# Spreading GpSimd's gathers and scatters over the expert items by due dates

## The chip, the cores and the metric

The kernel runs on one core of a Trainium2 chip. The metric is the device time of one execution in microseconds (us); three executions were timed, and their median is compared. A profiled execution gives the trace: what each engine did, and when. TensorE is PE, VectorE is DVE, ScalarE is ACT, GpSimd is POOL; SP only issues DMAs here.

## The reference, cut to what matters

Attention over 4 batches, 8 heads, 768 positions and 64 elements, in which a query sees the keys of its own cluster, is followed by a mixture of eight experts with one expert for each of the 3072 tokens:

```python
expert_idx = np.argmax(logits, axis=1)
gate_w = probs[np.arange(N), expert_idx]
for e in range(E):
    mask = expert_idx == e
    h = np.maximum(x[mask] @ w1[e], 0.0)
    out[mask] = gate_w[mask, None] * (h @ w2[e])
```

x has 512 columns, w1 is 512 x 1024 and w2 1024 x 512 for each expert, all in fp32.

## The kernel before, in words

The first half (to about 360 us) is attention. It writes x to DRAM (`x_rows`) and finds each token's expert and a place for it. The change touches only what follows: the experts.

The tokens are dealt to *items*, each with one expert's weights. Four "early" items (`E0`) take tokens of the first batches, 128 rows each. The list `later` has 16 more: later[0] is a "block" (128 rows), later[1] and later[2] are "sized", then block and sized alternate (sized ones are 1, 2, 4, 6, 8, 10, 12, 14), and later[15] is a block. The eight sized items hold up to 272, 256, 240, 224, 208, 192, 176 and 160 tokens (`CAPS`), in that order. Overflow items stand behind a branch (`overflow`) that is not taken with these inputs.

One item goes through these steps:

- **Weights.** `weights1` and `weights2` (L1117 to L1131) load w1 and w2, 2 MB each, on SP's queue into one of two buffers each, two items ahead.
- **Gather** (`fetch`, L1133). POOL issues indirect DMAs from `x_rows`, each of 128 pieces of 128 elements. A sized item has WIDE[j] of them (9, 8, 8, 7, 7, 6, 6, 5) into `xs` (two buffers), a block has four into `xin` (three buffers). The instruction is at L1079 inside `gather`.
- **Turn** (`turn_x`). DVE transposes `xs` to `xTs` (L1177) or `xin` to `xTm` (L1186).
- **Hidden.** `sized_hidden` (L1207): eight groups of matmuls (L1217) into PSUM banks, three of h_ps and one of x_ps (groups 4 and 8), each group evicted by ACT with a Relu to `hTs` (L1224). For a block `hidden` does it in two halves (L1303, L1310).
- **Result.** `sized_result` (L1243): four groups of matmuls (L1254) against `w2o`, a copy of w2 in another order that DVE made before (`order_w2`, L1202). DVE transposes each group into `ys` (L1263), and then multiplies `ys` by the gates in place (L1277). A block's result (L1319) is scaled by ACT to `y` (L1330), and POOL scatters it to `out` with one DMA.
- **Send** (`send`, L1281). POOL scatters a sized item's `ys` to `out` with WIDE[j] indirect DMAs (L1090 inside `scatter`). `ys` has two buffers.

Each engine runs its instructions in the order in which the program emits them; nothing is reordered. The loop at the end of the kernel (L1600 to L1642) writes that order by hand. In iteration i it turns the activations of later[i + 1], issues all gathers of later[i + 2] if that is sized, then the scatters of later[i - 1], then emits the hidden part of later[i]. The gathers of a following block wait on POOL behind a one-element copy (`pace`, L1628) of the last hidden group. Of the scatters of a sized item before a block, the first three (`RUN`) are issued at once, the rest behind a copy of the block's last hidden element (L1598). So POOL works in rows of seven to thirteen DMAs.

Of the kernel before, what the change touches and what calls it, by code (L numbers as in the profile page):

```python
# [9 lines left out]
F32 = mybir.dt.float32  # L10
# [8 lines left out]
P = 128  # L19

SQ = 32
# [18 lines left out]
def kernel(  # L40
# [12 lines left out]
    nc = tc.nc  # L53
# [4 lines left out]
    F = moe_w1.shape[2]  # L58
    N = B * S
# [5 lines left out]
    KF = F // P  # L65
    NQ = P // SQ
# [9 lines left out]
    WIDE = [-(-c // SQ) for c in CAPS]  # L76
    FIRST = [sum(WIDE[:i]) for i in range(E)]
# [1 line left out]
    NB = NS + KX  # L79


    RUN = 3
    MORE = (2, 4, 8)
    NO = sum(MORE)
    assert -(-(N - P - min(CAPS)) // P) <= KX + NO and min(CAPS) >= P
# [8 lines left out]
    x_pieces = x_rows.rearrange("n (w x) -> (n w) x", w=NQ)  # L94
    out_pieces = out.rearrange("n (w x) -> (n w) x", w=NQ)
# [57 lines left out]
    at = ctx.enter_context(ExitStack())  # L153
# [922 lines left out]
    mo = {}  # L1076

    def gather(to, of, at, n):
        nc.gpsimd.indirect_dma_start(  # L1079
            out=to,  # L1080
            out_offset=None,
            in_=of,
            in_offset=bass.IndirectOffsetOnAxis(ap=at, axis=0),
            bounds_check=n - 1,
            oob_is_err=False,
        )

    def scatter(to, at, of, n):

        inst = nc.gpsimd.indirect_dma_start(  # L1090
            out=to,
            out_offset=bass.IndirectOffsetOnAxis(ap=at, axis=0),
            in_=of,
            in_offset=None,
            bounds_check=n - 1,
            oob_is_err=False,
        ).ins
        tc.declare_no_dep(
            inst, group="out", reason="a row of out is written by one slot of one item"
        )  # L1100
        tc.add_to_no_dep_group("out", inst)
# [16 lines left out]
    def weights1(it, parts=1):  # L1118
        it.e = expert_of(it)
        for i in range(parts):  # L1120
            load_part(w1s[it.slot], moe_w1, it.e, KD, i, parts)

    def weights2(it, parts=1):
        for i in range(parts):
            load_part(w2s[it.slot], moe_w2, it.e, KF, i, parts)
# [4 lines left out]
            out=w[:, c], in_=x[ds(e, 1)].rearrange("o (c p) f -> p (o c) f", p=P)[:, c]  # L1130
        )  # L1131

    def fetch(it, a=0, z=None):  # L1133
        if a == 0:
            mo[it] = {}
        if it.kind == "sized":
            u0, n = FIRST[it.j], WIDE[it.j]
            if a == 0:
                mo[it]["xs"] = szp.tile([P, max(WIDE), P], F32, tag="xs", name="xs")
            xs = mo[it]["xs"]  # L1140
            for u in range(n)[a:z]:
                gather(xs[:, u], x_pieces, flat(gpidx)[:, u0 + u : u0 + u + 1], NQ * N)
            return
        if it.kind == "whole":
            xin = mo[it]["xin"] = it.xin
            gather(
                xin.rearrange("p w x -> p (w x)"), x_rows, it.tables[1][:, it.col : it.col + 1], N
            )
            return
        xin = mo[it]["xin"] = xip.tile([P, NQ, P], F32, tag="xin", name="xin")  # L1150
        if it.kind == "early":
            n = SA * P
            gather(
                xin.rearrange("p w x -> p (w x)"), x_rows[0:n], gidxs[0][:, it.j : it.j + 1], n
            )
            return
        for w in range(NQ):
            gather(xin[:, w], x_pieces, it.tables[0][:, it.col, w : w + 1], NQ * N)

    def fetch_gate(it):  # L1160
        gate = mo[it]["gate"] = xip.tile([P, 1], F32, tag="gatein", name="gatein", bufs=4)
# [42 lines left out]
                w2s[it.slot][:, f].rearrange("p (w g i) -> p g w i", w=NQ, i=SQ),  # L1204
            )

    def sized_hidden(it):  # L1207

        d, C = mo[it], CAPS[it.j]
        d["hT"] = szp.tile([P, KF, max(CAPS)], F32, tag="hTs", name="hTs", bufs=1)  # L1210
        for f in range(KF):
            if f % 4 == 3:
                bk = psX.tile([P, DM], F32, tag="x_ps", name="x_ps")[:, 0:C]
            else:
                bk = psH.tile([P, 512], F32, tag="h_ps", name="h_ps")[:, 0:C]
            for c in range(KD):
                nc.tensor.matmul(  # L1217
                    bk,
                    lhsT=w1s[it.slot][:, c, P * f : P * f + P],
                    rhs=d["xT"][:, c, 0:C],  # L1220
                    start=(c == 0),
                    stop=(c == KD - 1),
                )
            nc.scalar.activation(d["hT"][:, f, 0:C], bk, ACTF.Relu)  # L1224

    def spread_gates():

# [15 lines left out]
    def sized_result(it):  # L1243

        d, C, n = mo[it], CAPS[it.j], WIDE[it.j]
        ys = d["ys"] = szp.tile([P, max(WIDE), P], F32, tag="ys", name="ys")
        cut = KF - 2
        bks = {}

        def products(g, fs):  # L1250
            if g not in bks:
                bks[g] = misc() if g >= 2 else bank("y_ps", psY)
            for f in fs:
                nc.tensor.matmul(  # L1254
                    bks[g][:, 0:C],
                    lhsT=d["w2"][:, f, P * g : P * g + P],
                    rhs=d["hT"][:, f, 0:C],
                    start=(f == 0),
                    stop=(f == KF - 1),
                )  # L1260
# [12 lines left out]
        for g in range(2, KD):  # L1273
            products(g, range(KF))
            turn_back(g)
        u0 = FIRST[it.j]
        nc.vector.tensor_tensor(  # L1277
            ys[:, 0:n], ys[:, 0:n], bc(flat(gates4)[:, u0 : u0 + n], [P, n, P], 2), ALU.mult
        )

    def send(it, a=0, z=None):  # L1281

        u0, n = FIRST[it.j], WIDE[it.j]
        for u in range(n)[a:z]:
            at = flat(spidx)[:, u0 + u : u0 + u + 1]
            scatter(out_pieces, at, mo[it]["ys"][:, u], NQ * N)
        if z is None:
            del mo[it]

    def flat(t):  # L1290
        return t.rearrange("p k w -> p (k w)")
# [141 lines left out]
    with tc.manual_schedule(engines=by_hand):  # L1433
# [104 lines left out]
        gates = gate_pieces(B - 1, B)  # L1538
        gates[0]()
        result(E0[1], (1,))  # L1540
        pb.pieces(gpidx, spidx)
        fetch(later[0])
        pb.token_rows(None, sidxs[1])
# [50 lines left out]

        LAST = len(later) - 1

        def wait_hidden(it, f):
            nc.gpsimd.tensor_copy(pace, mo[it]["hT"][0:1, f : f + 1])  # L1598

        for i, it in enumerate(later):  # L1600
            if i == LAST - 1:
                overflow()
                weights1(later[LAST])
                weights2(later[LAST])
            if it.kind == "sized":
                order_w2(it)
            if i + 1 < len(later):
                turn_x(later[i + 1])
            if i > 0 and i + 2 < len(later) and later[i + 2].kind == "sized":
                fetch(later[i + 2])  # L1610
            late = i > 0 and later[i - 1].kind == "sized" and it.kind == "block" and i < LAST
# [4 lines left out]
            if it.kind == "sized":  # L1616
# [6 lines left out]
            if i == 0:  # L1623
                pb.gates(slot_gates)
            for j in range(i + 2, min(i + 4, len(later))):
                if later[j].kind == "block" and later[j] not in mo:
                    if it.kind == "sized":
                        nc.gpsimd.tensor_copy(pace, mo[it]["hT"][0:1, KF - 1, 0:1])  # L1628
                        fetch(later[j])
            if i + 2 < LAST:  # L1630
                weights1(later[i + 2])
                if it.kind == "sized":
                    weights2(later[i + 2])
            if it.kind == "sized":
                sized_result(it)
            else:
                result(it)
            if i == 0:
                fetch(later[2])
                spread_gates()  # L1640
            if i + 2 < LAST and it.kind != "sized":
                weights2(later[i + 2])  # L1642
        if later[-1].kind == "sized":
            send(later[-1])


# [41 lines left out]
```

## Time and profile before

| what | us |
|---|---|
| three executions | 699.18, 702.19, 703.92; median 702.19 |
| the profiled execution, its own time | 699.54 |
| its span in the trace | 697.7 |
| PE busy | 684.7 |
| POOL busy | 252.7 |
| POOL: 56 gathers to xs, 32 gathers to xin | 56.6 and 32.6 |
| POOL: 56 scatters of ys, 12 of y | 56.3 and 12.0 |
| POOL: copies to pace, 6 at L1598 and 7 at L1628 | 1.3 and 1.2 |

In the page's rows, "out<-in xcount | busy, mean ns | idle before, releaser" tells what a group of instructions writes and reads, how often, how long in all and on average, and how long its engine had been idle ahead of it, with what ended that. POOL's bar for an indirect DMA ends when the engine is done with issuing; the data lands later. In the table by stage each row gives a stage's limits and length, the busy time of PE, PE's weight loads, DVE, ACT and POOL (instructions in brackets), the granted PE clock, the share of time in which DMA engines were busy, and GB/s.

### The profile page before, as it was taken

How to read it: one execution, taken by the hardware profiler on the slowest of the kernel's cores; microseconds unless marked ns; L12 is line 12 of the kernel's file. 1: busy time of each engine (PE TensorE's matmuls, PEld its weight loads, DVE VectorE, ACT ScalarE, POOL GpSimd, SP SyncE). 2: the span in 40 equal slices, each digit the busy share in tenths (PEclk: the TensorE clock that was granted, in tenths of full speed). 3: DMA queues.
4: the chain of work that ended last, by engine and by line, in shares of the span. 5: the costliest groups of instructions: out<-in, count | busy, mean ns of one | idle time of the engine just before them, and what ended most of it. 6: DMA issues, size and time to landing. Idle time of an engine off the chain costs nothing.

```text
span 697.7 us, 16185 instructions
## 1 busy us (share of the span) xinstructions
PE 684.7 (98%) x6517; PEld 459.1 (66%) x6517; DVE 381.4 (55%) x667; ACT 261.5 (37%) x443; POOL 252.7 (36%) x439
## 2 busy tenths in 40 slices
PE   8999999999999999999999999998999999999996
PEld 4444444444444444456776678887979797979694
DVE  6788998998899999988563121240210303030310
ACT  5656655577666765576142120101010111111111
POOL 2122222321132222361216256736364554635402
PEclk9999999999999999999999999999999999999999
DMA  8755566875578587699699957457777686879450
GB/s 136 121 90 108 103 98 82 163 142 104 107 134 165 122 154 149 173 277 260 171 357 353 348 172 284 158 192 244 260 249 268 218 296 236 294 265 317 143 226 32
DMA packets 244156, 135.55 MB, mean 194 GB/s; under 512 B 207840, under 2 KB 207842, under 8 KB 244076
## 3 DMA queue, kind: packets, MB, share of 16 engines
q1 hardware_dynamic: 237116, 121.10, 63.9%
q0 software_dynamic: 6016, 13.12, 5.2%
q8 instruction: 54, 0.88, 0.6%
q10 hardware_dynamic: 944, 0.23, 0.2%
q14 instruction: 26, 0.21, 0.1%
HBM read 115.92 MB, written 13.12 MB: 185 GB/s over the span
## 4 chain that ended last, share of the span: by engine, by line
PE 89%; issue 4%; DMA 3%; POOL 1%; DVE 1%; another core or an unknown queue 1%; POOLq 0%; ACT 0%; DVEq 0%
PE s_ps L519 22%; PE o_ps L541 18%; PE h_ps L1303 10%; PE y_ps L1319 10%; PE h_ps L1217 9%; PE y_ps L1254 5%; PE misc L1254 5%; PE x_ps L1217 3%; DMA out_dram<-ys,spidx 3%; PE misc L591 2%; PE misc L412 2%; PE misc L670 1%; POOL out_dram L1090 0%; POOL xin L1079 0%
## 5 line engine op out<-in xcount | busy, mean ns | idle before, releaser
L530 ACT ACTIVATE prob<-s_ps 128x768 f32<-128x768 f32 x192 | 154.1, 814 | 100.8 <-PE s_ps L519 99.9
L519 PE MATMUL s_ps<-qT,kT 64*64 64x384 f32 x1536 | 155.6, 482 | 0.0
L541 PE MATMUL o_ps<-prob,v 64*64 64x385 f32 x1536 | 141.2, 483 | 0.0
L560 DVE TENSOR_TENSOR acc<-acc,prob 128x768 f32<-128x768 f32 x128 | 121.6, 950 | 8.5
L541 PEld LDWEIGHTS o_ps<-prob,v 64*64 64x64 f32 x1536 | 58.4, 133 | 65.0 <-issue 57.8
L1263 DVE STREAM_TRANSPOSE ys<-y_ps 128x256 f32<-128x256 f32 (+4 forms) x16 | 6.5, 414 | 156.8 <-PE y_ps L1254 141.1
L1303 PE MATMUL h_ps<-xTm,w1s 128*128 128x128 f32 x768 | 89.0, 276 | 1.2 <-issue 1.2
L1303 PEld LDWEIGHTS h_ps<-xTm,w1s 128*128 128x128 f32 x768 | 87.6, 192 | 3.0 <-issue 2.6
L1319 PE MATMUL y_ps<-w2s,hT 128*128 128x512 f32 x192 | 84.5, 593 | 0.0
L1090 POOL DMA_INDIRECT out_dram<-ys,spidx x56 | 56.3, 1005 | 74.7 <-DVE ys L1277 58.7
L519 PEld LDWEIGHTS s_ps<-qT,kT 64*64 64x64 f32 x1536 | 55.2, 133 | 36.9 <-issue 32.3
L1217 PE MATMUL h_ps<-xTs,w1s 128*128 128x272 f32 (+7 forms) x384 | 72.9, 346 | 1.1 <-ACTq L1577 1.1
L1217 PEld LDWEIGHTS h_ps<-xTs,w1s 128*128 128x128 f32 x384 | 66.6, 190 | 8.0 <-issue 2.4
L575 POOL COPY behind<-acc 1x1 f32<-1x1 f32 x30 | 6.7, 223 | 177.9 <-DVE acc L560 169.1
L1310 ACT ACTIVATE hT<-h_ps 128x512 f32<-128x512 f32 x24 | 14.3, 596 | 146.1 <-PE h_ps L1303 136.3
L519 PE MATMUL s_ps<-hot 64*64 64x384 bf16 x768 | 64.2, 325 | 1.0 <-DVE hot L478 0.7
L1079 POOL DMA_INDIRECT xs<-x_rows,gpidx x56 | 56.6, 1010 | 17.1 <-issue 16.8
L1319 PEld LDWEIGHTS y_ps<-w2s,hT 128*128 128x128 f32 x192 | 35.6, 190 | 40.2 <-issue 40.2
L519 PEld LDWEIGHTS <-hot 64*64 64x64 bf16 x768 | 23.8, 106 | 43.8 <-issue 41.8
L1254 PE MATMUL y_ps<-hTs,w2o 128*128 128x272 f32 (+7 forms) x256 | 48.2, 346 | 0.2 <-issue 0.2
L1254 PE MATMUL misc<-hTs,w2o 128*128 128x272 f32 (+7 forms) x256 | 48.0, 346 | 0.0
L1254 PEld LDWEIGHTS y_ps<-hTs,w2o 128*128 128x128 f32 x256 | 44.4, 190 | 2.9 <-issue 0.4
(273 smaller groups left out, 694.9 us busy)
## 6 DMA issues: line engine op xcount, KB each, us to landing
w1s<-in_moe_w_dram SPq DMA_DIRECT2D x18, 2048.0 KB
w2s<-in_moe_w_dram SPq DMA_DIRECT2D x18, 2048.0 KB
v<-in_v_dram SPq DMA_DIRECT2D x128, 48.0 KB
k<-in_k_dram SPq DMA_DIRECT2D x62, 96.0 KB
q<-in_q_dram SPq DMA_DIRECT2D x60, 96.0 KB
x_rows<-xb SPq DMA_DIRECT2D x60, 96.0 KB
xr<-x_rows SPq DMA_DIRECT2D x9, 512.0 KB
w1s<-in_moe_w_dram SPq DMA_DIRECT2D x4, 1024.0 KB
```

Of the source, the lines that this page charges most:

```text
L412: nc.tensor.matmul(bk[2 * C * i : 2 * C * i + 2 * C, 0:HS], lhsT=cnB[:, hp], rhs=r, start=True, stop=True,)
L519: nc.tensor.matmul(s_ps[D * half : D * half + D, h, 0:HS], lhsT=l[rows, half], rhs=r[rows], start=part == (1 if len(parts) < 2 else 0), st ...
L530: nc.scalar.activation(d["prob"][:, :, 0:HS], d["s_ps"][:, :, 0:HS], ACTF.Exp, scale=scale)
L541: nc.tensor.matmul(g["o_ps"][D * h : D * h + D, half, 0:HE], lhsT=ld[n]["v"][keys, j, h], rhs=d["prob"][keys, h, 0:HE], start=(j == 0), st ...
L560: nc.vector.tensor_tensor(g["acc"], g["acc"], d["prob"][:, :, 0:HS], ALU.add)
L1079: nc.gpsimd.indirect_dma_start(out=to, out_offset=None, in_=of, in_offset=bass.IndirectOffsetOnAxis(ap=at, axis=0), bounds_check=n - 1, oo ...
L1090: inst = nc.gpsimd.indirect_dma_start(out=to, out_offset=bass.IndirectOffsetOnAxis(ap=at, axis=0), in_=of, in_offset=None, bounds_check=n - 1,
L1217: nc.tensor.matmul(bk, lhsT=w1s[it.slot][:, c, P * f : P * f + P], rhs=d["xT"][:, c, 0:C], start=(c == 0), stop=(c == KD - 1),)
L1254: nc.tensor.matmul(bks[g][:, 0:C], lhsT=d["w2"][:, f, P * g : P * g + P], rhs=d["hT"][:, f, 0:C], start=(f == 0), stop=(f == KF - 1),)
L1303: nc.tensor.matmul(bk[:, m : m + P], lhsT=w1s[it.slot][:, c, f0 + m : f0 + m + P], rhs=d["xT"][:, P * c : P * c + P], start=(c == 0), stop ...
L1310: nc.scalar.activation(d["hT"][:, f0 : f0 + 512], bk, ACTF.Relu)
L1319: nc.tensor.matmul(bk, lhsT=d["hT"][:, P * c : P * c + P], rhs=w2s[it.slot][:, c], start=(c == 0), stop=(c == KF - 1),)
```

## The change

A list `queue` takes the place of the fixed rows. `fetches(it)` and `sends(it)` return one small job for each DMA instead of issuing them, and each job goes into the queue with a due date, the number of an iteration. The gathers of later[i + 2], if sized, and of the blocks later[i + 2] and later[i + 3] are due in iteration i; the scatters of later[i - 1] are due in i + 1. `share(i, left, x)` is called seven times in a sized item (after hidden groups 2, 4, 6 and 8, and after result transposes 1, 2 and 3) and three times in a block (ahead of the hidden part and after each half). It issues the number of due jobs divided by the chances left in this item, or a smaller share of all jobs if that is more. `pump` puts one copy of an element of x (of `hTs`, `hT` or `ys`) into `pace` on POOL ahead of the lot. The last iterations send the rest. The parts of later[1] and later[2] are queued in the same way, the former among the early items.

The core of the diff:

```diff
-    RUN = 3
...
+    def fetches(it):
+
+        d = mo.setdefault(it, {})
+        if it.kind == "sized":
+            to, u0 = szp.tile([P, max(WIDE), P], F32, tag="xs", name="xs"), FIRST[it.j]
+            d["xs"], at, n = to, flat(gpidx)[:, u0:], WIDE[it.j]
+        else:
+            to = d["xin"] = xip.tile([P, NQ, P], F32, tag="xin", name="xin")
+            at, n = it.tables[0][:, it.col], NQ
+        return [
+            lambda u=u: gather(to[:, u], x_pieces, at[:, u : u + 1], NQ * N) for u in range(n)
+        ]
...
             nc.scalar.activation(d["hT"][:, f, 0:C], bk, ACTF.Relu)
+            then(f, d["hT"][0:1, f, 0:1])
...
+            then(g, ys[0:1, 0, SQ * g : SQ * g + 1])
...
+        def pump(n, behind=None):
+            if n and queue and behind is not None:
+                nc.gpsimd.tensor_copy(pace, behind)
+            queue.sort(key=lambda j: j[0])
+            for due, job in queue[0:n]:
+                job()
+            del queue[0:n]
+
+        def share(i, left, behind=None):
+
+            due = len([j for j in queue if j[0] <= i])
+            pump(max(-(-due // left), -(-len(queue) // (left + 3))), behind)
...
-        fetch(later[1], 0, NQ)
+        for job in jobs_of(later[1], 0)[0:NQ]:
+            job()
         result(E0[2])
-        fetch(later[1], NQ)
+        pump(2)
         weights2(later[0])
         turn_x(later[0])
         result(E0[3])
+        pump(1)
...
             if i > 0 and later[i - 1].kind == "sized":
-                send(later[i - 1], 0, RUN if late else None)
-                if i == LAST:
-                    nc.gpsimd.drain()
-            if it.kind == "sized":
-                sized_hidden(it)
+                made = mo[later[i - 1]]["ys"][0:1, 0, 0:1]
+                queue.extend((min(i + 1, LAST - 2), f) for f in sends(later[i - 1]))
+            if 0 < i < LAST - 1 and later[i + 2].kind == "sized":
+                jobs_of(later[i + 2], i)
+            for k in range(i + 2, i + 4):
+                if wide and block(k) and later[k] not in mo:
+                    jobs_of(later[k], i)
+            if wide:
+                sized_hidden(it, lambda f, x: share(i, 7 - f // 2, x) if f % 2 else None)
...
+                sized_result(it, lambda g, x: share(i, 3 - g, x) if g < 3 else None)
+            elif i < LAST:
+                share(i, 3, made)
+                hidden(it, (0,))
+                share(i, 2, mo[it]["hT"][0:1, 511:512])
+                hidden(it, (1,))
+                share(i, 1, mo[it]["hT"][0:1, F - 1 : F])
...
             else:
+                pump(len(queue))
+                nc.gpsimd.drain()
                 hidden(it)
-            if late:
-                wait_hidden(it, F - 1)
-                send(later[i - 1], RUN)
...
-                    if it.kind == "sized":
-                        nc.gpsimd.tensor_copy(pace, mo[it]["hT"][0:1, KF - 1, 0:1])
-                        fetch(later[j])
```

More of the change, by code (lines that the diff above doesn't have):

```diff
@@ L1131, in load_part, with fetch @@
         )
-    def fetch(it, a=0, z=None):
-        if a == 0:
-            mo[it] = {}
-        if it.kind == "sized":
[L1137 to L1143, printed above, removed]
+    def fetch(it):
+        mo[it] = {}
         if it.kind == "whole":
@@ L1205, in order_w2, with sized_hidden @@
             )
-    def sized_hidden(it):
+    def sized_hidden(it, then=lambda f, x: None):
         d, C = mo[it], CAPS[it.j]
@@ L1241, in spread_gates, with sized_result @@
         nc.vector.tensor_tensor(gates4, gates4, parts[:, 2], ALU.add)
-    def sized_result(it):
+    def sized_result(it, then=lambda g, x: None):
         d, C, n = mo[it], CAPS[it.j], WIDE[it.j]
@@ L1279, in sized_result, with sends @@
         )
[L1281 to L1288, printed above, removed]
+    def sends(it):
+        u0, ys = FIRST[it.j], mo.pop(it)["ys"]
+        return [
+            lambda u=u: scatter(
+                out_pieces, flat(spidx)[:, u0 + u : u0 + u + 1], ys[:, u], NQ * N
+            )
+            for u in range(WIDE[it.j])
+        ]
     def flat(t):
@@ L1540, with jobs_of @@
         result(E0[1], (1,))
+        queue = []
+        def jobs_of(it, due):
+            jobs = fetches(it)
+            queue.extend((due, f) for f in (jobs[NQ:] if due == 0 else jobs))
+            return jobs
+        def pump(n, behind=None):
[8 more added lines that the diff above has]
+            pump(max(-(-due // left), -(-len(queue) // (left + 3))), behind)
         pb.pieces(gpidx, spidx)
@@ L1595, with block @@
         LAST = len(later) - 1
-        def wait_hidden(it, f):
-            nc.gpsimd.tensor_copy(pace, mo[it]["hT"][0:1, f : f + 1])
+        def block(k):
+            return k <= LAST and later[k].kind == "block"
         for i, it in enumerate(later):
@@ L1604 @@
                 weights2(later[LAST])
-            if it.kind == "sized":
+            wide = it.kind == "sized"
+            if wide:
                 order_w2(it)
-            if i + 1 < len(later):
+            if i > 1 and i + 1 < len(later):
                 turn_x(later[i + 1])
-            if i > 0 and i + 2 < len(later) and later[i + 2].kind == "sized":
-                fetch(later[i + 2])
-            late = i > 0 and later[i - 1].kind == "sized" and it.kind == "block" and i < LAST
+            made = None
@@ L1612 @@
             if i > 0 and later[i - 1].kind == "sized":
-                send(later[i - 1], 0, RUN if late else None)
-                if i == LAST:
-                    nc.gpsimd.drain()
-            if it.kind == "sized":
-                sized_hidden(it)
-            else:
+                made = mo[later[i - 1]]["ys"][0:1, 0, 0:1]
+                queue.extend((min(i + 1, LAST - 2), f) for f in sends(later[i - 1]))
+            if 0 < i < LAST - 1 and later[i + 2].kind == "sized":
+                jobs_of(later[i + 2], i)
@@ new lines @@
+            for k in range(i + 2, i + 4):
+                if wide and block(k) and later[k] not in mo:
+                    jobs_of(later[k], i)
+            if wide:
+                sized_hidden(it, lambda f, x: share(i, 7 - f // 2, x) if f % 2 else None)
+                if i == 1:
+                    turn_x(later[2])
+                if i + 2 < LAST:
+                    weights1(later[i + 2])
+                    weights2(later[i + 2])
+                sized_result(it, lambda g, x: share(i, 3 - g, x) if g < 3 else None)
[5 more added lines that the diff above has]
+                share(i, 1, mo[it]["hT"][0:1, F - 1 : F])
+                if i == 0:
+                    turn_x(later[1])
+                    pb.gates(slot_gates)
+                if i + 2 < LAST:
+                    weights1(later[i + 2])
+                result(it)
+                if i == 0:
+                    jobs_of(later[2], 1)
+                    spread_gates()
+                if i + 2 < LAST:
+                    weights2(later[i + 2])
+            else:
+                pump(len(queue))
+                nc.gpsimd.drain()
@@ L1619 @@
                 hidden(it)
-            if late:
-                wait_hidden(it, F - 1)
-                send(later[i - 1], RUN)
[L1623 to L1627, printed above, removed]
-                        nc.gpsimd.tensor_copy(pace, mo[it]["hT"][0:1, KF - 1, 0:1])
-                        fetch(later[j])
[L1630 to L1633, printed above, removed]
@@ L1634 @@
-            if it.kind == "sized":
-                sized_result(it)
-            else:
-                result(it)
[L1638 to L1644, printed above, removed]
+                result(it)
 _INS = [
```

## The prediction

> **What bounds the kernel now.** I read the page first, then the busy time by stage, then what TensorE (PE) waited for stage by stage, and last the timeline of the one place where it waited. The first row of the page, and two stages of the expert part from the table by stage:
>
> ```profile
> PE 684.7 (98%) x6517; PEld 459.1 (66%) x6517; DVE 381.4 (55%) x667; ACT 261.5 (37%) x443; POOL 252.7 (36%) x439
> ```
>
> ```profile
> 440.00:473.00 33.00, 33.00 (x170) 27.12 (x170) 8.45 (x19) 2.73 (x6) 18.93 (x21) 1.00 0.58 208
> 473.00:516.00 43.00, 40.87 (x211) 34.79 (x210) 7.63 (x16) 4.53 (x11) 20.88 (x24) 1.00 0.68 236
> ```
>
> The second number after the stage is its length, the third PE's busy time. PE is idle for 13.0 us of the 697.7 us span. About 6.3 of these lie around the last matmuls (660 to 698), 1.16 at 389 to 392 (PE's own issue), 1.1 at the branch of the overflow (659.4 to 660.5). GpSimd (POOL) is about half busy in the expert part, so what the change reorders is not the bound; it matters only where something it feeds reaches PE late. The chain of waits runs through POOL from 636 us on; there I follow PE instead, which works on without a gap, because POOL waits there for DVE and ACT. All waits of PE from 402 to 660:
>
> ```profile
> PE x_ps L1217 <- ACT hTs L1224: 2.1, 1, 2.1
> PE y_ps L1254 <- issue: 0.2, 1, 0.2
> ```
>
> The 2.1 us are in later[4], a sized item. Timeline of ACT, POOL and PE there (start, duration, then idle time before it):
>
> ```profile
> 475.37 0.37 ACT L1224 ACTIVATE hTs<-h_ps 128x240 f32<-128x240 f32 x1 [0.99 <-issue]
> 478.82 0.37 ACT L1224 ACTIVATE hTs<-h_ps 128x240 f32<-128x240 f32 x1 [3.08 <-PE h_ps L1217]
> 482.42 0.37 ACT L1224 ACTIVATE hTs<-h_ps 128x240 f32<-128x240 f32 x1 [3.23 <-PE h_ps L1217]
> 486.70 0.37 ACT L1224 ACTIVATE hTs<-x_ps 128x240 f32<-128x240 f32 x1 [3.91 <-remote]
> ...
> 475.95 1.04 POOL L1079 DMA_INDIRECT xs<-x_rows,gpidx  x1 [0.30 <-issue]
> ...
> 483.83 1.00 POOL L1079 DMA_INDIRECT xs<-x_rows,gpidx  x1 [0.30 <-issue]
> ...
> 487.12 1.89 PE L1217 MATMUL x_ps<-xTs,w1s 128*128 128x240 f32 x8 [2.13 <-ACT hTs L1224]
> ```
>
> PE had finished the first four of the eight hidden groups at 475.3, 476.9, 478.5 and 480.1 (eight matmul records, 1.62 us, each). ACT evicts the first at once, the next three 1.9, 3.9 and 6.6 us late, and the eighth group, which needs x_ps back, stops PE. ACT catches up 1.9 us after the last of seven gathers in a row, issued while the w2s load of 473.68 runs. In later[6] the same happens (gathers 518.3 to 527.2, ACT up to 5.5 us late, free at 529.1), where the buffers hide nearly all of it. In later[1], with gathers but the load over by 408, ACT is on time; so it is beside the 438 to 449 scatters. What delays it I cannot see; that it goes with a long row of gathers inside a weight load I can.
>
> [...] a gather issued at 385.67 to 386.67 beside w2s loads was turned by DVE at 392.98, 6.3 us on, and one that ended at 415.12 on idle queues at 416.75, 1.6 us on. [...] so POOL's 1.0 us bars say nothing of landing. [...] Here a scatter beside w2o's copies takes 1.12 us instead of 0.97; the trace decides, so I price it at 0.15.
>
> **The change part by part.** In after's instruction order PE, DVE, ACT and SP keep every instruction in place; only POOL's order changes. Matmuls, bytes and SP's weight loads stay.
>
> *Removed:* seven waits on hTs and six on hT with their bursts behind. *Added:* 68 pace copies for 13, so 55 more: 0.18 us each, with the idle time beside it about 0.6, 33 us of POOL in 300. A DMA costs POOL 1.3 us from start to start (1.00 + 0.30). In the worst pair of items, later[4] and [5], there are 23 DMAs and 10 copies: 23 x 1.3 + 10 x 0.6 = 36 us in the pair's 42.3 (473.49 to 515.82). In the last pair, [12] and [13], 19 and 10: 31 in 34.2. POOL keeps up; cost on PE 0. Without that cover each us too much per pair would add itself.
>
> *Moved gathers.* I replayed POOL with these prices against the trace's ACT and DVE times. The ninth gather of later[1] goes from 386.98 to behind hT of later[0] (ACT ends at 392.2), so it ends about 394.4 instead of 387.98. At the 6.2 us that it took before it lands at 400.6; DVE turns it (0.31), then its four gate operations (0.9) end at 401.8. PE needs the gates' copy at 402.20 and xTs at 402.41. Cost 0 with 0.6 to 1.5 us in hand, bound 0 to +3. later[2]'s last gather ends at 421.3 instead of 415.1, beside the w1s and w2s loads of 417.4; with 3 to 6 us of landing, 425 to 428, before 431.85. For the other items the last xs gather ends 5 us or more ahead of DVE's turn.
>
> *New wait.* ys is read by the pace copies, and the gate multiply (L1277) writes ys in place, so it now also waits for POOL. In the replay the copy behind the third transpose runs at 464.5 for later[2] and 506.6 for later[4]; the multiply was here:
>
> ```profile
> 460.16 1.22 DVE L1277 TENSOR_TENSOR ys<-ys,gates 128x1024 f32<-128x1024 f32 x1
> 461.30 1.30 DVE L1177 STREAM_TRANSPOSE xTs<-xs 128x512 f32<-128x512 f32 x2
> ```
>
> So it slips 4.4 and 4.1 us, in later items 1 to 2. Queued behind it on DVE are the transpose to xTs (1.3), w2o (2.9) and xTm (0.7); later[4]'s xTs is ready at about 467.1 and PE wants it at 473.5, later[6]'s at 508.9 for 515.8. Slack 6.4 and 6.9 us, later 9 to 10. PE's banks come free by the transposes ahead of the multiply. Cost 0, hidden by the block item's 14 us; bound 0 to +7.
>
> *The lag of ACT.* In later[4]'s hidden part POOL now issues six scatters, and its seven xs gathers move to 493 and after, into the result part, where a late DVE has slack. In later[6] about three DMAs fall before the eighth group, mostly scatters. So I take the 2.1 us and the 0.2 away: -2.4 us with the 0.1 by which x_ps matmuls are stretched. Bounds: 0 (the lag moves with the traffic) to -5, if the other executions, 2.65 us above the profiled one, hold more of it. I take -2.4, the amount the trace shows.
>
> *Tail.* later[13] sends all that is left; later[14] and [15] issue as before, the drain included. Cost 0.
>
> Sum: 697.7 - 2.4 = 695.3 us of span, with the 1.84 us around it (699.54 - 697.7) 697.1 for a profiled execution. The median of the runs, 702.19, is 2.65 above the profiled 699.54; I keep that distance: **699.8 us**.
>
> **Rivals.** *No gain:* scatters and gathers still share the DMA engines with the loads, and every sized item still has POOL work in its hidden part; the lag comes up elsewhere or stays. For it: DVE was 4.9 us late in later[2]'s result part as well, beside four gathers. Against it: scatters alone left ACT on time. 702.2 us. It includes that the change spreads less than it says: POOL is so full around 460 to 510 that lots run into each other. *First gather late:* the ninth gather needs 9 us instead of 6.2; PE starts later[1] up to 3 us late, 705.2 us. *Slower, by the new wait:* POOL's copies wait for ACT and DVE and inherit their lag. The multiply of later[2] may slip 6.4 us more before PE stops; one lag of 6.6 us, ACT's worst, costs 0.2, two in one result part 13.2 - 6.4 = 6.8 us, which gives 709.0 us. Each further pair that does so adds as much. Against it: slack grows to 9 to 10 us later. *More gain:* all of the 2.65 us goes too, 697.1 us or, with the 1.16 at 389 to 392, 695.9.
>
> **How the numbers follow.** Chances: my forecast 0.52, no gain 0.27, first gather late 0.09, slower by the wait 0.07, more gain 0.05. The range is 695.5 to 706.0: the forecast with its bound of -5 at the lower end and the spread of the runs (699.18 to 703.92), no gain and the late gather inside, the slower case left out. Beyond 1% (7 us), about what a measurement of this kernel can tell from no change, on the fast side would take more than the idle time of PE that the change can reach (2.4 + 1.2 + 1.1 = 4.7) and something unseen besides: 0.04, taken out of the more-gain case. On the slow side the wait's case and a little of the late gather: 0.08. Within: 0.88. The forecast itself lies within 1%.
>
> **What would show it.** Right: in the waits of PE the line for hTs is gone or under 1 us; ACT's evictions in later[4] and [6] follow PE by 0.1 us; the multiply at L1277's place waits for a POOL copy by 2 to 5 us in later[2] and [4], and PE goes from item to item without a gap. Wrong: a wait of PE for the transposes of xs or for the gates' copy before later[1] (the first gather), one for xTs at 473 or 516 (the new wait), or ACT late by 4 us and more in other sized items (no gain). A time under 695 or over 709 would say that my reading of PE as the bound missed a stage.

## The result, and the profile after

| what | before | after |
|---|---|---|
| executions, us | 701.07 median (697.60 to 703.92, 6 runs) | 694.87 median (694.68 to 695.32, 6 runs) |
| profiled execution, its own time, us | 699.54 | 695.09 |
| its span in the trace, us | 697.7 | 693.3 |
| POOL: pace copies; busy us | 13; 252.7 | 68; 266.2 |

The changed kernel takes 0.9923 of the time before, 95% interval [0.9896, 0.9951]: 6.2 us less, 4.9 below the predicted 699.8 and a little below the range, but inside 1%. Its executions lie 0.64 us apart, those of the kernel before 6.3. The kernel before takes 694.5 us in some sessions and 696 to 702 in others (a session is a set of runs made one after the other on one chip), so each experiment below stands beside runs of the kernel before from its own session. The chip doesn't tell these sessions apart: e9 and e11, in one of each kind, both ran on the one numbered 15. One of the four runs of e12 (720.66 us), 1.6% above the fastest of its kernel, is left out of its numbers.

The first row of the page after, and the two stages shown of before:

```profile
PE 684.1 (99%) x6517; PEld 459.3 (66%) x6517; DVE 381.8 (55%) x667; ACT 262.6 (38%) x443; POOL 266.2 (38%) x494
```

```profile
440.00:473.00 33.00, 33.00 (x170) 26.97 (x169) 7.76 (x16) 3.03 (x6) 20.80 (x28) 1.00 0.61 218
473.00:516.00 43.00, 43.00 (x226) 37.64 (x226) 7.51 (x16) 5.56 (x13) 27.05 (x35) 1.00 0.73 258
```

PE's busy time is nearly the same (684.7 and 684.1); of the 4.4 us by which the span is shorter, 3.8 are idle time of PE. From 473 to 516 PE was busy 40.87 us of 43 and is now busy all 43. In that stage POOL has more to do than before (27.05 us for 20.88). All waits of PE from 360 us to the end of the span:

```profile
PE h_ps L1220 <- ACTq L1605: 1.1, 1, 1.1
```

That is the branch of the overflow, there before as well. The wait for hTs and the small one of y_ps are gone. ACT in later[4]'s hidden part, from the timeline:

```profile
475.24 0.37 ACT L1227 ACTIVATE hTs<-h_ps 128x240 f32<-128x240 f32 x1 [1.19 <-PE h_ps L1220]
476.86 0.37 ACT L1227 ACTIVATE hTs<-h_ps 128x240 f32<-128x240 f32 x1 [1.25 <-PE h_ps L1220]
478.48 0.37 ACT L1227 ACTIVATE hTs<-x_ps 128x240 f32<-128x240 f32 x1 [1.25 <-PE x_ps L1220]
...
486.46 0.37 ACT L1227 ACTIVATE hTs<-x_ps 128x240 f32<-128x240 f32 x1 [2.75 <-remote]
```

The evictions follow at PE's step of 1.62 us; only the eighth comes late, by 1.5 us. "remote" is a release that the trace has no record of. ACT is not on time everywhere: in the block later[7] the first half is evicted 2.6 us late, which lengthens that part on PE by 0.1 us:

```profile
542.30 0.60 ACT L1316 ACTIVATE hT<-h_ps 128x512 f32<-128x512 f32 x1 [17.91 <-remote]
```

The gain has a second part that I had not forecast, ahead of later[1]. PE in later[0]'s hidden part, before and then after:

```profile
385.42 4.07 PE L1303 MATMUL h_ps<-xTm,w1s 128*128 128x128 f32 x35
389.95 0.27 PE L1303 MATMUL h_ps<-xTm,w1s 128*128 128x128 f32 x1 [0.46 <-issue]
390.68 0.49 PE L1303 MATMUL h_ps<-xTm,w1s 128*128 128x128 f32 x2 [0.46 <-issue]
391.40 3.16 PE L1303 MATMUL h_ps<-xTm,w1s 128*128 128x128 f32 x26 [0.24 <-issue]
```

```profile
385.56 7.31 PE L1309 MATMUL h_ps<-xTm,w1s 128*128 128x128 f32 x64
```

The same 64 matmuls took 9.1 us (385.42 to 394.56) and take 7.3. So later[1] starts on PE at 400.7 instead of 402.4 (1.7 us), later[6] at 511.7 instead of 515.8 (2.4 more), later[14] at 656.0 instead of 660.5 (0.4 more). That is the 4.4 us of the spans.

### The profile page after: what moved, and what is told of

It is laid out like the page before. It is cut to its first block, busy times and chain, and to the rows that moved or that the text cites. A ratio compares the mean times of both kernels' runs of the same rounds, so it can differ in the third digit from the quotient of the medians.

```text
span 693.3 us, 16291 instructions
## 1 busy us (share of the span) xinstructions
PE 684.1 (99%) x6517; PEld 459.3 (66%) x6517; DVE 381.8 (55%) x667; ACT 262.6 (38%) x443; POOL 266.2 (38%) x494
## 4 chain that ended last, share of the span: by engine, by line
PE 91%; issue 3%; DMA 3%; POOL 1%; DVE 1%; POOLq 0%; ACT 0%; DVEq 0%
PE s_ps L518 22%; PE o_ps L540 18%; PE h_ps L1309 10%; PE y_ps L1325 10%; PE h_ps L1220 9%; PE y_ps L1258 6%; PE misc L1258 5%; PE x_ps L1220 3%; DMA out_dram<-ys,spidx 3%; PE misc L590 2%; PE misc L411 2%; PE misc L669 1%; PE idle_ps L232 1%; POOL xin L1078 0%; POOL out_dram L1089 0%
## 5 line engine op out<-in xcount | busy, mean ns | idle before, releaser
L1258 PEld LDWEIGHTS misc<-hTs,w2o 128*128 128x128 f32 x256 | 44.4, 190 | 2.7 <-issue 0.2
```

The costliest lines, as they stand in the source:

```text
L1258: nc.tensor.matmul(bks[g][:, 0:C], lhsT=d["w2"][:, f, P * g : P * g + P], rhs=d["hT"][:, f, 0:C], start=(f == 0), stop=(f == KF - 1),)
```

## The experiments

Lateness of ACT or DVE is worked out from the trace: start of the eviction or transpose less the end of PE's group. A "row" is a run of POOL's indirect DMAs with less than 0.6 us from the end of one to the start of the next, counted in POOL's timeline. "The lag" is the lateness of ACT, DVE and PE that the kernel before shows in some sessions.

### e1 to e4: four ways to part the change, in a session without the lag

e1 is the kernel before with the xs gathers of later[4] and each sized item after it taken out of the hidden part and put behind a copy of the last hidden group:

```diff
             if i + 1 < len(later):
                 turn_x(later[i + 1])
-            if i > 0 and i + 2 < len(later) and later[i + 2].kind == "sized":
-                fetch(later[i + 2])
...
             if i == 0:
                 pb.gates(slot_gates)
+            if i > 0 and i + 2 < len(later) and later[i + 2].kind == "sized":
+                nc.gpsimd.tensor_copy(pace, mo[it]["hT"][0:1, KF - 1, 0:1])
+                fetch(later[i + 2])
```

> The kernel before, with one edit: the gathers of the sized item two ahead are issued in one row behind the last hidden group instead of ahead of the first. Rows stay long (seven gathers, then the four of the block), nothing is spread, the row among the early items stays. Theory (place): a row of gathers inside a weight load holds up the engines beside it, and it costs only where PE depends on ACT soon, in the hidden part; moved out of it, ACT is on time (0.1 us) in later[4] and later[6], the 2.4 us of PE's idle time there go, the 1.2 to 1.8 us at later[0] stay, and DVE is late by up to 5 us in the result parts instead. Span about 695, time 0.3 to 0.7% below before. Rival (length of the row): only short lots cure it; with eleven in a row it gets worse, ACT or DVE late by 5 us or more, PE waits again for hTs or for xTs: no gain, within 0.2% of before.

e2 is the kernel before with these gathers left in the hidden part, but in lots of two behind every second hidden group:

```diff
+            then(f)
...
-            if i > 0 and i + 2 < len(later) and later[i + 2].kind == "sized":
-                fetch(later[i + 2])
...
+                def lot(f):
+                    if f % 2 and i > 0 and i + 2 < len(later) and later[i + 2].kind == "sized":
+                        nc.gpsimd.tensor_copy(pace, mo[it]["hT"][0:1, f, 0:1])
+                        fetch(later[i + 2], f - 1, f + 1)
+
+                sized_hidden(it, lot)
```

> The kernel before, with one edit: the gathers of the sized item two ahead stay in the hidden part but go out in lots of two, each behind a copy of hidden group 2, 4, 6 or 8. Theory (place): inside the w2 load of the block it is the same traffic at nearly the same time, so ACT is still late by 2 us or more in later[4] or later[6], and PE still waits for hTs: within 0.3% of before. Rival (length of the row): lots of two behind ACT cannot run ahead of it, ACT is late by under 1 us, PE's wait for hTs is gone: 0.3 to 0.7% below before.

e3 is the changed kernel with later[1]'s last five gathers in one row again (`pump(2)` becomes `pump(len(queue))`, the `pump(1)` goes):

> The changed kernel, but with the gathers of later[1] as before: four, then five in one row ahead of the scatter of the last early item. Theory: the gaps of PE in later[0]'s hidden part (1.8 us in the trace of before, none in that of the changed kernel) come from that row; they are back, span 694.5 to 695.5, time 0.2 to 0.3% above the changed kernel, and the spread of its runs grows. Rival: the gaps came by chance and not by that row: span 693.3 as in the changed kernel.

e4 is the kernel before without the loads of w2 for later[5], [7], [9], [11] and [13]; it leaves these weights out, so part of the computation works on old ones:

```diff
-            if i + 2 < LAST and it.kind != "sized":
+            if i + 2 < LAST and it.kind != "sized" and i < 3:
                 weights2(later[i + 2])
```

> The kernel before, but the w2 of the block items later[5], [7], [9], [11] and [13] is not loaded (their results are computed with the w2 that is in the buffer); these five loads ran beside the hidden part of a sized item. Rows of gathers stay. Theory (a row of gathers hurts only inside a weight load): ACT is on time, within 0.2 us, in the hidden parts of later[4] to later[12], and PE's wait for hTs is gone: span about 695, 0.3 to 0.5% below before. Rival (the row alone does it, without a load): ACT is late by 2 us or more in later[4] and later[6] as before, and the time within 0.2% of it.

Measured: before 694.50 (41 runs); e1 694.43, ratio 1.0 [0.9992, 1.0009]; e2 694.52, 0.9999 [0.999, 1.0007]; e3 694.61, 1.0 [0.9992, 1.0009]; e4 694.30, 0.9996 [0.9987, 1.0004]. Here the kernel before had no lag to lose, so none of the four tells the theories apart. They do show two things: without the lag the order of POOL's work is worth nothing either way, to 0.1%, and the changed kernel's 694.87 us has nearly reached the 694.5 of the kernel before without the lag. As e4 met no lag, the part of the weight loads stays untested by it.

### e5 and e6: the changed kernel again, and rows made longer

e5 is the changed kernel as it is. e6 is the kernel before with the first four gathers of later[4] and of each sized item after it issued twice, the second time into a spare tile; these rows grow by four, no weight load moves:

```diff
+            if it.j >= 2:
+                again = szp.tile([P, NQ, P], F32, tag="again", name="again", bufs=1)
             for u in range(n)[a:z]:
-                gather(xs[:, u], x_pieces, flat(gpidx)[:, u0 + u : u0 + u + 1], NQ * N)
+                at = flat(gpidx)[:, u0 + u : u0 + u + 1]
+                gather(xs[:, u], x_pieces, at, NQ * N)
+                if it.j >= 2 and u < NQ:
+                    gather(again[:, u], x_pieces, at, NQ * N)
```

> The changed kernel once more, unaltered, beside the kernel before. In the four runs ahead of this one the kernel before took 694.5 us instead of 701.1, with no late ACT in the traces beside it, so what held it up was not there. Theory (the change only takes away the exposure to a lag that is there at some times or on some chips): where the kernel before takes 697 us or more, this one is 0.5 to 1% below it; where it takes 694.5, the two agree within 0.1%. Rival (the change takes a constant amount): 0.4% or more below before in either case.

> The kernel before, but the first four gathers of later[4] and of each later sized item are issued twice, the second time into a spare tile: rows of nine to twelve DMAs instead of five to eight at the start of the hidden part, the result unchanged. Theory (a row only hurts where the lag is there): where the kernel before takes 694.5 us, nothing, within 0.15%, since PE waits for nothing on POOL; where it takes 697 us or more, ACT is late for longer and the time is 0.3% or more above it. Rival (the length of the row makes the lag by itself): ACT is late by 2 us or more in the hidden parts in either case, and PE waits for hTs.

Measured: before 701.71 (698.25 to 703.15, 7 runs); e5 694.92 (694.79 to 695.19), ratio 0.9909 [0.9876, 0.9942]; e6 729.13 (727.08 to 730.55), ratio 1.0386 [1.0348, 1.0424]. PE's largest waits in e6 from 360 us on, and the worst place (ACT, then PE):

```profile
PE h_ps L1222 <- issue: 10.2, 1, 10.2
PE x_ps L1222 <- issue: 5.7, 2, 3.5
PE y_ps L1259 <- issue: 3.3, 5, 0.9
PE h_ps L1222 <- ACT hTs L1229: 1.8, 1, 1.8
```

```profile
448.36 0.38 ACT L1229 ACTIVATE hTs<-h_ps 128x256 f32<-128x256 f32 x1 [30.88 <-remote]
```

```profile
436.73 1.89 PE L1222 MATMUL x_ps<-xTs,w1s 128*128 128x256 f32 x8
448.80 3.78 PE L1222 MATMUL h_ps<-xTs,w1s 128*128 128x256 f32 x8 [10.18 <-issue]
```

PE had finished this first hidden group at 433.4; ACT evicts it 14.9 us later, and the second one 18.8 us late. PE's fifth group needs a bank of h_ps back and starts at 448.80, as this eviction ends. A row of 16 gathers ran on POOL from 418 to 438.8, and nine scatters after a pause of 0.94 us. From 432 to 450 no weights were being loaded; the queue of SP (q1) beside that of POOL (q0) in the table of DMA queues for this stretch (packets, MB, share of the 16 engines' time):

```profile
q0 software_dynamic: 434, 0.87, 15.7%
q1 hardware_dynamic: 5, 0.01, 0.1%
```

So the largest lateness in all traces falls where no weight load runs, and a pause of 0.94 us does not end it once it is there. That a load has no part in it isn't shown: this row ran beside one up to 432, and so did every row longer than nine in the traces with the lag for about half of its time or more (worked out from q1's packets). The rows of nine that ran without a load, all of scatters (e6, e11 and e12), had engines at most 1.2 us late beside them in e11 and e12; in e6 the lag was there already. Two dozen more DMAs (six items of four) cost 27 us, with POOL busy for 275.3 us of a span of 728.7.

### e7, e8, e9: again without the lag

e7 is e2, e8 is e1 once more. e9 is the changed kernel without its copies to pace: queue and due dates stay, so the lots run into one another.

```diff
         def pump(n, behind=None):
-            if n and queue and behind is not None:
-                nc.gpsimd.tensor_copy(pace, behind)
             queue.sort(key=lambda j: j[0])
```

> The kernel before with the gathers of the sized item two ahead kept in the hidden part, in lots of two behind hidden groups 2, 4, 6 and 8, once more: on the chip of the first try the kernel before had no lag to cure. With doubled rows, on a chip where it has, ACT was 15 us late while SP's queue was empty, so a weight load is not needed; the length of GpSimd's rows is my theory now. Theory (row length), where the kernel before takes 697 us or more: ACT is late by under 1 us in later[4] and later[6], PE's wait for hTs is gone, time 0.4 to 0.9% below before, though the gathers stay in the hidden part. Rival (place): ACT late by 2 us or more there, within 0.3% of before. Where the kernel before takes 694.5 us neither is told apart.

> The kernel before with the same gathers in one row of up to twelve behind the last hidden group, once more. Theory (row length), where the kernel before takes 697 us or more: the lag is as large or larger than in before, now in the result part: DVE or ACT late by 3 us or more there, PE partly held up, time from 0.5% below to 1% above before. Rival (place): the lag is harmless there, 0.4 to 0.9% below before, as the changed kernel.

> The changed kernel without the copies to pace: the same lots in the same order, but GpSimd issues them as soon as it reaches them, so they run together into rows and run ahead into the hidden part. Theory (rows without a pause make the lag), where the kernel before takes 697 us or more: ACT is late by 2 us or more in some sized item, 0.3% or more above the changed kernel's 694.9. Rival (the order and the due dates do it, not the copies): within 0.15% of 694.9.

Measured: before 694.59 (31 runs); e7 694.53, ratio 0.9999 [0.9991, 1.0008]; e8 694.50, 1.0 [0.9991, 1.0009]; e9 694.49, 0.9999 [0.9990, 1.0007]. Inconclusive again for the cause, but useful as a pair to e11: e9 has a row of 34 DMAs (401 to 446), and neither ACT nor DVE is over 0.11 us late in these items.

### e10: lots of two in the hidden part, with the lag there

The kernel of e2.

> The kernel before with the gathers of the sized item two ahead in lots of two inside the hidden part, a third time, because both chips it ran on took 694.5 us for the kernel before, with nothing to cure. Where the kernel before takes 697 us or more: theory (the length of GpSimd's rows makes the lag): ACT late by under 1 us in later[4] and later[6], PE's wait for hTs gone, 0.3% or more below before; not all of the changed kernel's 0.9%, as the row at later[0] and the rows of scatters stay. Rival (gathers in the hidden part do it, however they are spread): ACT late by 2 us or more there, within 0.3% of before.

Measured: before 696.10 (695.93 to 697.12, 7 runs); e10 704.54 (703.45 to 706.53), ratio 1.0127 [1.0108, 1.0147]. Slower, yet the trace holds both answers in one execution. In later[4] POOL pauses between the lots; its timeline, then ACT's there:

```profile
484.40 0.18 POOL L1618 COPY pace<-hTs 1x1 f32<-1x1 f32 x1 [1.78 <-ACT hTs L1224]
485.15 1.06 POOL L1079 DMA_INDIRECT xs<-x_rows,gpidx  x1 [0.58 <-issue]
486.52 1.01 POOL L1079 DMA_INDIRECT xs<-x_rows,gpidx  x1 [0.31 <-issue]
487.64 0.18 POOL L1618 COPY pace<-hTs 1x1 f32<-1x1 f32 x1
488.36 1.03 POOL L1079 DMA_INDIRECT xs<-x_rows,gpidx  x1 [0.54 <-issue]
489.69 1.00 POOL L1079 DMA_INDIRECT xs<-x_rows,gpidx  x1 [0.30 <-issue]
```

```profile
487.13 0.37 ACT L1224 ACTIVATE hTs<-x_ps 128x240 f32<-128x240 f32 x1 [1.25 <-PE x_ps L1217]
488.75 0.37 ACT L1224 ACTIVATE hTs<-h_ps 128x240 f32<-128x240 f32 x1 [1.25 <-PE h_ps L1217]
490.37 0.37 ACT L1224 ACTIVATE hTs<-h_ps 128x240 f32<-128x240 f32 x1 [1.25 <-PE h_ps L1217]
```

The gathers stand where they stood in the kernel before, in the hidden part and beside the loads, and ACT is never over 0.12 us late here or in any later sized item. In later[2] the copies' groups were long done when POOL reached them: nine scatters, eight gathers to xs and four to xin ran as a row of 21 from 433 to 461. DVE came 12.4 us late, and PE went in single matmuls:

```profile
456.92 0.47 PE L1255 MATMUL misc<-hTs,w2o 128*128 128x256 f32 x1 [1.04 <-issue]
457.62 0.41 PE L1255 MATMUL misc<-hTs,w2o 128*128 128x256 f32 x1 [0.23 <-issue]
459.02 1.20 PE L1255 MATMUL misc<-hTs,w2o 128*128 128x256 f32 x2 [1.00 <-issue]
460.40 0.59 PE L1255 MATMUL misc<-hTs,w2o 128*128 128x256 f32 x1 [0.18 <-issue]
```

Later[4] to later[14] take 183.9 us from start to start, as in e2 without the lag (183.9); of the 8.7 us by which the span is longer than e2's (701.6 and 692.9), 7.8 are lost between the starts of later[1] and later[4]. So gathers in the hidden part are harmless in short lots, and a long row brings the lag back.

### e11: due dates without the copies, with the lag there

The kernel of e9.

> The changed kernel without the copies to pace, a second time, hoping for a chip on which the kernel before is slowed. On the chip of the lots in the hidden part ACT was on time in every item where the lots had pauses between them, and DVE was 12 us late in later[2], where nine scatters, eight gathers and four more gathers ran together. Where the kernel before takes 695.5 us or more: theory (a row without pauses makes the lag, whatever is in it): without the copies the lots run together into rows of ten and more, ACT or DVE is late by 3 us or more in two items or more and PE loses time: 0.3% or more above 694.9. Rival (due dates and order are what counts): no gap of PE, 694.9 within 0.15%.

Measured: before 696.50 (696.37 to 697.15, 7 runs); e11 735.78 (733.50 to 739.98), ratio 1.0568 [1.0525, 1.0611]. Rows are 25, 18, 15, 14, 14 and 13 long. The two traces of this one kernel, with POOL issuing the same DMAs at the same times to within 0.1 us from 401 to 434; PE and DVE first in e9, then in e11:

```profile
422.83 7.50 PE L1258 MATMUL misc<-hTs,w2o 128*128 128x272 f32 x32
430.16 5.34 PE L1220 MATMUL h_ps<-xTs,w1s 128*128 128x256 f32 x24
```

```profile
426.55 1.46 PE L1258 MATMUL misc<-hTs,w2o 128*128 128x272 f32 x3 [1.01 <-issue]
428.69 0.82 PE L1258 MATMUL misc<-hTs,w2o 128*128 128x272 f32 x1 [0.68 <-issue]
430.10 0.61 PE L1258 MATMUL misc<-hTs,w2o 128*128 128x272 f32 x1 [0.59 <-issue]
431.51 1.33 PE L1258 MATMUL misc<-hTs,w2o 128*128 128x272 f32 x2 [0.80 <-issue]
```

```profile
437.29 0.85 DVE L1267 STREAM_TRANSPOSE ys<-y_ps 128x288 f32<-128x288 f32 x2 [21.51 <-remote]
```

In e11 PE resumes at 428.69, 430.10 and 431.51, 1.41 us apart, close to POOL's 1.31 us from DMA to DMA, and DVE's first transpose of this item comes 15.2 us late. ACT's last two evictions of this item's hidden part were late before that, by 2.1 and 3.1 us, between two weight loads (q1 moves next to nothing from 410 to 419):

```profile
415.94 0.40 ACT L1227 ACTIVATE hTs<-h_ps 128x272 f32<-128x272 f32 x1 [3.47 <-PE x_ps L1220]
418.81 0.40 ACT L1227 ACTIVATE hTs<-x_ps 128x272 f32<-128x272 f32 x1 [2.47 <-remote]
```

In each of the six sized items beside which a row begins, ACT is on time for the first five groups and over 2 us late from the seventh, six to ten DMAs into the row. Due dates without the copies are 39 us worse than the kernel before, so the copies bring the gain. The changed kernel itself did not run beside e11; in the two sessions with the lag where it did run, it never took more than 695.32.

### e12: the place moved, the row kept

The kernel of e1.

> The kernel before, with the xs gathers of every later sized item taken out of the hidden part and issued in one row behind the copy of the last hidden group, with the xin gathers behind them: up to eleven gathers without a pause, all in the result part. Where the kernel before lies near 694.5 us in the same call, it tells nothing and gives 694.5. Where before is above 696: if the place decides (gathers in the hidden part, where ACT's lag reaches PE soon, as the prediction had it), ACT follows PE by 0.1 us in the hidden parts, DVE is late in the result parts and has slack there, PE doesn't wait, and the time is that of the changed kernel, about 694.9. If the row's length decides, the row of eleven makes DVE and PE late in the result part too, with waits of PE that the trace calls issue: as long as before or longer, 698 to 715 us.

Measured: before 700.67 (698.14 to 703.72, 7 runs); e12 710.19 (709.60 to 711.42, 3 runs), ratio 1.0139 [1.0085, 1.0193]. ACT follows PE by 0.04 to 0.12 us in the hidden parts of the sized items, with one exception of 0.53: the lag has left them. It is now in the result parts and the next block:

```profile
PE h_ps L1303 <- issue: 8.9, 17, 1.2
PE h_ps L1217 <- ACTq L1577: 1.1, 1, 1.1
PE y_ps L1319 <- ACT hT L1310: 0.2, 1, 0.2
```

The rows of 9 to 12 in the result parts make DVE 2.7 to 8.4 us late, ACT up to 5.6 us late in the blocks, and stretch the block's hidden part. Behind the row of 12 (447 to 463) alone, later[2] to later[4] took 47.2 us from start to start for 41.6 in e1. So moving a row doesn't remove the lag. But the place decides who is late and what that costs: in the kernel before the row of 13 from 438 to 455, which starts in the hidden part of the same item, made DVE 4.9 us late and cost PE nothing (41.6 us from later[2] to later[4]). And with rows that are no longer than those of the kernel before, e12's span is 15.8 us above that of e1, the same kernel without the lag, where that of the kernel before is 5.2 above. In the sessions with the lag the changed kernel is the only version that beats the kernel before; e1 and e2, at 694.4 to 694.5, ran without it.

## Why the prediction was right, and where its steps failed

A small gain, within 1%, was forecast, and one came; but 2.4 us of gain were forecast and 6.2 measured. That it stayed within 1% is in part luck: the interval reaches 1.04%, in e5's session the gain was 0.91%, and in a session without the lag there is next to nothing to gain. The prediction's own sign of a missed stage, "a time under 695", came as well (694.87). The stage that it missed is later[0]'s hidden part.

**PE is the bound, and only idle time can be won.** Right: PE's busy time stayed within 0.6 us, and the 4.4 us of span are idle and stretched time of PE.

**POOL keeps up.** Right: 55 more copies cost PE nothing that its waits show. That POOL keeps to the order of the program shows in the trace of before: the eight gathers of later[2], which stand behind a scatter of y in the program, start at 404.69, 0.31 us after that scatter, which had waited 14.01 us for ACT. (The last pair of items lasts 34.4 us, 626.08 to 660.45, not 34.2.)

**The ninth gather of later[1].** In time, as said, but sooner: I put its end at 394.4; it was issued at 390.91, with a bar of 1.02 us on POOL, and DVE turned it at 396.27, four us ahead of PE. The end of hT's half, behind which it waits, had moved forward: in the kernel before, ACT evicted that half 2.5 us late. By the prediction's own figures 0.4 to 1.5 us were in hand, not 0.6 (402.20 less 401.8). later[2]'s last gather, too, was turned at 424.2, before the forecast 425 to 428.

**The new wait of the gate multiply.** There, as said, and hidden, but mis-sized: a slip of 4.4 and 4.1 us was forecast for later[2] and later[4]. The row of DVE's waits after:

```profile
DVE ys L1282 <- POOL pace L1556: 3.7, 4, 1.5
```

It is 3.7 us over four items, 1.5 at most, 0.54 in later[4] and none in later[2]. My replay took DVE's and ACT's times from the trace of before, with the lag in them.

**The lag of ACT, -2.4 us.** The size was right for the stage (2.4 between the starts of later[1] and later[6]). It was the wait that the trace of before showed, so it would have fitted any reason for which the wait goes. The reason given was only half right. It had two parts, place and load: "it goes with a long row of gathers inside a weight load I can" say, and the gathers "move to 493 and after, into the result part". They did move, to 484.21 and after. But e12 moves them as far and loses about 10 us, and e10 leaves them in the hidden part, beside the loads, and later[4] loses nothing. The reading of "seven gathers in a row" was short as well: they are the end of a row of 13 that begins with six scatters, ahead of the item's hidden part. The first and the last of the six:

```profile
468.29 0.98 POOL L1090 DMA_INDIRECT out_dram<-ys,spidx  x1 [0.57 <-issue]
474.68 0.97 POOL L1090 DMA_INDIRECT out_dram<-y,sidx  x1 [0.30 <-issue]
```

What brings the lag, in the sessions that have it, is how many indirect DMAs POOL issues without a pause: e6 lengthens six rows by four gathers and loses 27 us, e11 only takes the copies away, without one DMA more, and loses 39. In the kernel before the rows are 16, 9, 12, 13, 13, 13, 7, 7 and 6 long; behind the row of 16 PE stutters at 389 to 392, behind 12 and 13 DVE or ACT is 3.8 to 6.6 us late, behind 9 and less never more than 2.0. In the changed kernel the longest are 12 (368 to 384, after which PE runs on without a gap) and twice 11, with copies among them; ACT is at most 1.5 us late in the sized items and 2.6 in the blocks, and DVE 1.8. (DVE's 2.7 us in later[1] are not the lag: they are there in e3 without it, because DVE waits for later[2]'s last gather first.) e5 has 2.2, 2.7 and 1.8. The length has no sharp threshold: behind rows of nine to eleven in e12 DVE was 2.7 to 4.3 us late, behind rows of 11 in the changed kernel at most 1.8. Most copies inside those rows of 11 copy something already done, and leave 0.34 us between two DMAs instead of 0.30. So the count alone doesn't tell the lateness.

**The step that failed: "1.16 at 389 to 392 (PE's own issue)".** The sum put it at nothing, as PE's own. It was the lag too, behind a row of 16, and it went with the rest: 1.7 us, since the matmuls beside the gaps were stretched too. That the row makes it, e3 was to show, but it met no lag. The other traces with the lag show it: where the row of 16 stands there (before, e6, e10, e12), later[0]'s hidden part takes 9.1, 8.8, 8.3 and 9.2 us; where that row is 12 long (after, e5, e11), it takes 7.3 each time. PE in e12 there:

```profile
385.36 4.18 PE L1303 MATMUL h_ps<-xTm,w1s 128*128 128x128 f32 x36
390.63 0.27 PE L1303 MATMUL h_ps<-xTm,w1s 128*128 128x128 f32 x1 [1.08 <-issue]
391.32 3.28 PE L1303 MATMUL h_ps<-xTm,w1s 128*128 128x128 f32 x27 [0.43 <-issue]
```

**The distance of 2.65 us to the median.** I kept it; it went. No trace of the other executions is kept; that they held more of the lag is argued from the spread: 697.6 to 703.9 before, 694.68 to 695.32 after, and 0.7 us for the kernel before in the session of e1 to e4, without the lag. Against 699.8 the sum is short by 2.0 in the span (695.09 for 697.1) and by 2.9 in the distance (-0.2 for 2.65), 4.9 in all. The rival "more gain" named both and was given 0.05. With a row that explains all late engines, it should have had more.

**What stays open.** How POOL's rows hold up other engines is not settled, nor whether a weight load or the kind of DMA (gathers or scatters) has a part in it: no long row ran wholly without a load. A slowing of POOL's own packets isn't seen: from 401 to 446 a packet of its queue takes 0.106 us on average in e9 and 0.102 in e11. PE stops inside a group of matmuls on operands it has: in e11 its gaps begin at 423.95, and w2o had been written by 404.77 and hTs by 419.21 (ends of DVE's and ACT's last instructions on them). That speaks against a semaphore from POOL's side as the only cause. Instruction fetches seem not to be it: the only packet of the queue of kind "instruction" from 400 to 445 took 1.05 us in e11 and 1.04 in e9. Nor is it known why the lag is there in some sessions and not in others: e9 and e11, one kernel, are 41 us apart.

## What to carry to other kernels

When several engines show small waits called "issue" or "remote" at once, look at what GpSimd is doing then, and count how many indirect DMAs it issues without a pause. If rows are longer than six to ten (in e11 ACT was over 2 us late that far into a row) and engines are late beside them, break them into lots of two or three behind copies that really wait for something recent (e10, later[4]: ACT at most 0.12 us late); a copy of something long done (e10, later[2]: 0.34 us between two DMAs, DVE 12.4 us late) is no pause, and moving the row elsewhere (e12) makes another engine late (DVE up to 8.4 us), at a higher cost here. Look at the spread of the executions before you keep their distance to the profiled one: here 6.3 us between the runs of one kernel became 0.64 in the changed one.

## What the runs showed of the hardware that was not expected

One 128-piece indirect DMA per 1.3 us on POOL, in rows of up to 17 (e6) or 25 (e11), made ACT up to 18.8 us (e6) and DVE up to 15.2 us late (e11) and cost 27 and 39 us of the kernel's time, or nothing (e9, the program of e11). The sessions with the lag have a mark in their traces, worked out by counting the records of semaphores that DMAs raise. Up to 360 us all fourteen traces have 5998 to 6044. After it, the seven traces from sessions without the lag have 2931 to 3020, and the seven from sessions with it 1227 to 1655, the changed kernel's too (1564 and 1530) though it is not slowed. One sees it in the views as well; DMA issues from 400 to 445 in e9 and in e11, with the median time to landing as last number where the records allow one:

```profile
xs<-x_rows,gpidx POOLq DMA_INDIRECT x16, 5.5
xin<-x_rows,gpidx POOLq DMA_INDIRECT x8, 3.5
```

```profile
xs<-x_rows,gpidx POOLq DMA_INDIRECT x16
xin<-x_rows,gpidx POOLq DMA_INDIRECT x8
```

After 360 us, then, about half of these records are missing where the lag is. Why, and whether the late engines have to do with it, is not shown: no run here tested it. One thing follows for reading these traces: where records are missing, "issue" and "remote" can hide a releaser that was there. For the last eviction of later[1]'s hidden part the trace of e9 names PE's x_ps (415.70) and that of e11 "remote" (418.81); for one gather of POOL e9 names the DMA of xs (411.14) and e11 "issue" (411.19).
